# Local attention with a phase mixer on one core: constants in two parts, key reorders on ScalarE, and the order of values, scores and weight transposes

## The chip, the core and the metric

The kernel runs on one core of a Trainium2 chip. The metric is the device time in microseconds of one execution; lower is better. TensorE (PE in the profile) multiplies matrices into PSUM, VectorE (DVE) and ScalarE (ACT) do elementwise work, GpSimd (POOL) issues the loads, SyncE (SP) issues the stores and the transposing DMAs.

## The reference

Four batches, 8 heads, 768 positions, 64 numbers a head. First comes an attention with a local window and eight global positions, then a token and channel mixer on its output.

```python
scores = q @ k.T / sqrt(64)                       # per batch and head
keep   = (col < 8) | ((row - col >= 0) & (row - col < 96))
dist   = where((col < 8) & ~local, 96, |row - col|)
scores = where(keep, scores - slope[head] * dist, -1e9)
x      = softmax(scores) @ v                      # heads side by side: 768 x 512
theta  = x @ w_theta
y      = w_tok_r @ (x * cos(theta)) + w_tok_i @ (x * sin(theta))
u      = x + y
out    = u + relu(u @ w_ch)
```

## The kernel before

Heads are taken in four pairs, and the 768 positions in six tiles of 128. Matmul operands are bf16, sums are float32 in PSUM. There are two large PSUM buffers (`ps_big`, two banks each) and four small ones (`ps_small`), which are handed out in turn.

**Loads.** POOL issues all loads and converts them on the way: q and k of batch 0 by pairs (L72), v of batch 0 in two halves (L78), then `w_theta`, the six blocks of the two token matrices (L158), `w_ch`, then q, k and v of batches 1, 2 and 3. Tile `vn` holds v and, in a 65th column of each head, ones, so that the values' matmul also gives the softmax's sums. `alloc_loads` (L63) writes that column with a DVE memset ahead of the loads.

**Constants.** DVE builds a ramp, the identity `ident`, the distances `dist` with a huge number where the window doesn't reach, zeroes in four score buffers `e_0` to `e_3`, the mask and bias of the global columns (`gmask`, `gbias`), the shift matrices, pi/2, and `zero`, the operand of filler matmuls (`warm`, L174). ACT makes `etab`, the window's factors exp(-slope * dist), one exponential for each of eight heads (L110).

**Attention of a pair.** `prep` (L190) reorders q and k on DVE into `qkn` (two copies, L199), transposes them on PE (L207) and copies the results to `qT` by DVE (L212) and `kT` by ACT (L214). `scores` (L235) works on two tiles at a time (L247), takes the exponential on ACT (L251, L258, L259) and multiplies by `etab` on DVE (L254, L260, L261). `globals_` (L217) does the global columns of all pairs; `vglob` (L266) brings the global rows of v into place, with an ACT copy `vg` (L272). `values` (L275) sums both parts (L292) and divides on DVE (L300, L302) into `x_sb`. `xtrans` (L304) transposes x: on PE with an ACT copy in batch 0 (L312, L313), by a transposing DMA in the others (L306).

**Mixer.** `theta` (L318) multiplies x by `w_theta` (L327), two tiles to a large buffer; ACT takes both sines (L331, L332; cosine is the sine with pi/2 added), DVE multiplies them with x into `zri` (L335). `mix` (L340) runs 12 matmuls for each of six row tiles (L346), and DVE adds x to give u (L351). `utrans` transposes u by DMA (L360), `chan` multiplies by `w_ch` (L371), adds (L374) and stores (L376). The token matrices must stand transposed: `trans_w` (L163) does a row block of both, 12 transposes (L167) and two copies (L168).

**Order.** Batch 0's attention is written out for PE in a fixed order (L424 to L446): preparation of pair p, then scores of pair p-1, each chunk with a filler matmul, globals, the last pair's scores, then values of each pair. Between the values, W blocks 0 to 3 are transposed. After that come theta and mix of batch b, into which `weave` (L406) mixes the attention of batch b+1 by weights; W blocks 4 and 5 are transposed in batch 0's mixing (L463). Outside the fixed stretch a scheduler sets the order on each engine, from its own estimate of times. Each engine works through its queue in that order.

Of the kernel before, what the change touches and what calls it, by code (L numbers as in the profile page):

```python
# [9 lines left out]
FP = mybir.dt.float32  # L10
BF = mybir.dt.bfloat16
# [5 lines left out]
def kernel(  # L17
# [45 lines left out]
    def alloc_loads(b):  # L63
        qk = ld.tile([T, 2, H, NT, D], BF, name="qk")
        vn = ld.tile([T, H, NT, D + 1], BF, name="vn")
        nc.vector.memset(vn[:, :, :, D:D + 1], 1.0)
        loads[b] = (qk, vn)
# [17 lines left out]
    load_v(0, 0, 4)  # L85
    load_v(0, 4, 4)

    ones = const.tile([T, W], FP)
# [14 lines left out]
    far = const.tile([T, W], FP)  # L103
    nc.vector.tensor_scalar(far, dist, 0.0, 1e6, op0=ALU.is_lt, op1=ALU.mult)
    nc.vector.tensor_add(dist, dist, far)
    nc.vector.tensor_scalar(far, dist, float(NL), 1e6, op0=ALU.is_ge, op1=ALU.mult)
    nc.vector.tensor_add(dist, dist, far)
    etab = const.tile([T, H, W], BF)
    for h in range(H):
        nc.scalar.activation(etab[:, h, :], dist, AF.Exp, scale=-slopes[h])  # L110


    NE = 4
    e_bufs = []
    for i_ in range(NE):
        e_t = const.tile([T, 2, NT, 2 * T], BF, name=f"e_{i_}")
        nc.vector.memset(e_t[:, :, :, W:2 * T], 0.0)
        e_bufs.append(e_t)
    e_cnt = [0]

    grel = const.tile([T, T], FP)
    nc.vector.tensor_scalar(grel, ramp[:, 0:T], kmod[:, 0:1], None, op0=ALU.subtract)
    gbias = const.tile([T, 2], FP)
    for hh in range(2):
        for p in range(NP):
            nc.vector.memset(gbias[GS * p:GS * (p + 1), hh:hh + 1], -float(NL) * slopes[2 * p + hh])

    gneg = const.tile([T, 1], FP)  # L130
    nc.vector.tensor_scalar(gneg, grel[:, 0:1], -float(NG), -30000.0, op0=ALU.is_le, op1=ALU.mult)
    nc.vector.tensor_scalar(gbias, gbias, gneg, None, op0=ALU.add)

    gfar = const.tile([T, T], FP)
    nc.vector.tensor_scalar(gfar, grel, float(NL), None, op0=ALU.is_ge)
    gmask = const.tile([T, T], BF)
    nc.vector.scalar_tensor_tensor(gmask, in0=grel, scalar=0.0, in1=gfar, op0=ALU.is_lt, op1=ALU.add)

    shift = const.tile([T, NP, T], BF)
    nc.vector.memset(shift, 0.0)  # L140
    for p in range(NP):
        nc.vector.tensor_copy(out=shift[0:NG, p, GS * p:GS * p + NG], in_=ident[0:NG, 0:NG])

    halfpi = const.tile([T, 1], FP)
    nc.vector.memset(halfpi, HALF_PI)

# [22 lines left out]


    zero = const.tile([T, 512], BF)
    nc.vector.memset(zero, 0.0)  # L172

# [16 lines left out]
    def prep(b, p):  # L190
# [6 lines left out]
        with behind("dve"):  # L197
            for i_ in range(2):
                nc.vector.tensor_copy(out=qkn[:, :, i_].rearrange("p t h d -> p h t d"),  # L199
                                      in_=qk[:, i_, 2 * p:2 * p + 2])  # L200
        qT = att.tile([T, S], BF, name="qT", bufs=6)
# [33 lines left out]
    def scores(b, p, c):  # L235
# [14 lines left out]
        if jt + 2 < NT:  # L250
            nc.scalar.activation(  # L251
                e_t[:, :, jt:jt + 2, 0:W],
                pb[:, :, 0:2 * W].rearrange("p a (j w) -> p a j w", j=2), AF.Exp, scale=scale)
# [194 lines left out]
    for b in range(B):  # L448
# [61 lines left out]
```

The softmax here doesn't subtract the row's maximum and nothing guards it: scores larger than these inputs give would overflow.

## Time and profile before

Three runs gave 200.63, 201.6 and 202.19 us, with a median of 201.6.

| What | Value |
|---|---|
| profiled execution, device time | 201.24 us |
| its span | 199.5 us |
| busy: PE, DVE, ACT, POOL | 173.0, 132.6, 105.0, 27.2 us |
| first scores exponential of batch 0 (L251) | at 14.23 us |
| first sine of batch 0 (`cs`, L331) | at 38.72 us |
| first u of batch 0 to the transposing DMA | at 47.10 us |
| first `chan` matmul (L371) | at 54.46 us |
| first theta matmul of batch 1 (L327) | at 79.99 us |

The page gives busy time by engine, the slices of the span, the DMA queues, the chain of work that ended last, and the costliest groups of instructions. A row of a timeline has the start in us, the length in us, engine, line, operation, what is written from what, the count, and in brackets how long the engine had idled and what ended that. A matmul of 512 columns is shown with 0.38 us but starts every 0.216 us, since matmuls overlap. DMA rows on POOL and SP show the issuing only; the time to landing is told by another view.

### The profile page before, as it was taken

Reading aid. Unit: us, or ns where it says so; the run is one execution under the profiler, and the core shown is the slowest. Engines: PE = TensorE matmul, PEld = TensorE weight load, DVE = VectorE, ACT = ScalarE, POOL = GpSimd, SP = SyncE. Lnnn points to the kernel's source line nnn. Section 1 sums busy time; section 2 is a strip of 40 time slices with the busy share of each in tenths; the row PEclk is TensorE's granted clock in tenths of the full one; section 3 lists DMA queues with packets and bytes.
Section 4 is the critical chain, followed back from the end, with each engine's and each line's share of the span. In section 5 each row is a group of like instructions: output and inputs, shape, how many; then the busy total and the mean of one; then the engine's idle time right before and its main releaser. Section 6 shows DMA issues by size and latency. Waiting matters only on the chain.

```text
span 199.5 us, 3940 instructions
## 1 busy us (share of the span) xinstructions
PE 173.0 (87%) x1610; PEld 87.1 (44%) x1610; DVE 132.6 (66%) x305; ACT 105.0 (53%) x153; POOL 27.2 (14%) x31
## 2 busy tenths in 40 slices
PE   0498789998599899799999999699999997899981
PEld 0154268443353445453345455443444552344430
DVE  7878678177765686996676777677686661753332
ACT  2449956990359553189964431399845312920010
POOL 7991461040110000400000000000000000000000
PEclk9999999999999999999999999999999999999999
DMA  4999999999999999699114437210233845103432
GB/s 66 161 174 168 210 209 206 205 176 166 194 165 188 210 162 183 116 135 138 30 26 118 122 92 108 40 69 37 55 82 100 111 120 123 53 20 100 130 91 105
DMA packets 61345, 24.76 MB, mean 124 GB/s; under 512 B 47504, under 2 KB 58256, under 8 KB 61328
## 3 DMA queue, kind: packets, MB, share of 16 engines
q0 software_dynamic: 35760, 12.85, 66.0%
q1 hardware_dynamic: 25568, 11.67, 26.8%
q8 instruction: 12, 0.20, 0.4%
q14 instruction: 5, 0.04, 0.1%
HBM read 25.69 MB, written 6.29 MB: 160 GB/s over the span
## 4 chain that ended last, share of the span: by engine, by line
PE 61%; DMA 13%; ACT 12%; DVE 9%; issue 3%; ACTq 0%
PE ps L346 27%; DMA uT<-u 11%; PE ps L371 9%; PE pb L327 6%; PE pb L292 6%; PE pb L247 4%; PE ps L207 3%; ACT kT L214 2%; DMA xT<-x_sb 2%; PE ps L177 2%; ACT cs L331 2%; DVE u L351 1%; ACT e_121 L251 1%; PE ps L292 1%; PE ps L167 1%
## 5 line engine op out<-in xcount | busy, mean ns | idle before, releaser
L346 PE MATMUL ps<-zri,w_tokT_151 128*128 128x512 bf16 x144 | 53.9, 380 | 1.2 <-DVE zri L335 1.2
L346 PE MATMUL ps<-zri,w_tokT_152 128*128 128x512 bf16 x144 | 54.0, 379 | 0.1
L374 DVE SCALAR_TENSOR_TENSOR o_sb<-ps,u 128x512 f32<-128x512 f32 x24 | 16.5, 688 | 18.8 <-PE ps L371 18.8
L371 PE MATMUL ps<-w_ch_bf,uT 128*128 128x512 bf16 x96 | 24.7, 379 | 4.1 <-DMA uT<-u 3.3
L327 PE MATMUL pb<-w_theta_bf,xT 128*128 128x512 bf16 x96 | 24.6, 379 | 3.3 <-DMA xT<-x_sb 3.0
L214 ACT COPY kT<-ps 128x768 bf16<-128x768 bf16 x16 | 12.4, 808 | 25.9 <-PE ps L207 25.9
L335 DVE TENSOR_TENSOR zri<-x_sb,cs 128x512 bf16<-128x512 bf16 x48 | 18.2, 421 | 8.8 <-ACT cs L331 7.2
L346 PEld LDWEIGHTS <-w_tokT_151 128*128 128x128 bf16 x144 | 14.0, 97 | 16.9 <-issue 4.4
L351 DVE TENSOR_TENSOR u<-x_sb,ps 128x512 bf16<-128x512 bf16 x24 | 16.4, 684 | 7.0 <-PE ps L346 6.7
L346 PEld LDWEIGHTS <-w_tokT_152 128*128 128x128 bf16 x144 | 14.0, 98 | 12.8 <-issue 2.0
L247 PE MATMUL pb<-qT,kT 64*128 64x224 bf16 x192 | 16.8, 254 | 1.7 <-ACT e_117 L251 0.5
L212 DVE COPY qT<-ps 128x768 bf16<-128x768 bf16 x16 | 14.9, 948 | 2.5 <-PE ps L207 2.5
L177 PE MATMUL ps<-zero 128*128 128x512 bf16 x22 | 8.9, 476 | 8.3 <-DVE zero L172 7.8
L207 PE MATMUL ps<-ident,qkn 128*128 128x128 bf16 x192 | 13.8, 223 | 2.0 <-DVE qkn L199 2.0
L78 POOL DMA_DIRECT2D vn<-in_v_dram x5 | 10.2, 2050 | 35.7 <-DVE rec L300 24.7
L327 PEld LDWEIGHTS <-xT 128*128 128x128 bf16 x96 | 8.8, 98 | 14.1 <-DMA xT<-x_sb 4.1
L207 PEld LDWEIGHTS <-qkn 128*128 128x128 bf16 x192 | 12.1, 100 | 6.4 <-DVE qkn L199 3.8
L371 PEld LDWEIGHTS <-uT 128*128 128x128 bf16 x96 | 8.2, 97 | 14.7 <-DMA uT<-u 6.0
L247 PEld LDWEIGHTS <-kT 64*128 64x128 bf16 x192 | 6.0, 94 | 18.2 <-issue 15.8
L331 ACT ACTIVATE cs<-pb,halfpi 128x1024 bf16<-128x1024 f32 x12 | 13.6, 1131 | 0.5 <-ACT cs L332 0.3
L332 ACT ACTIVATE cs<-pb 128x1024 bf16<-128x1024 f32 x12 | 12.5, 1039 | 0.0
L199 DVE COPY qkn<-qk 128x768 bf16<-128x768 bf16 x32 | 11.5, 411 | 0.8 <-DMA qk<-in_q_dram 0.5
(128 smaller groups left out, 261.8 us busy)
## 6 DMA issues: line engine op xcount, KB each, us to landing
out_dram<-o_sb SPq DMA_DIRECT2D x24, 256.0 KB, 2.2
qk<-in_q_dram POOLq DMA_DIRECT2D x3, 768.0 KB, 17.5
qk<-in_k_dram POOLq DMA_DIRECT2D x3, 768.0 KB, 21.8
vn<-in_v_dram POOLq DMA_DIRECT2D x3, 768.0 KB, 23.3
w_nat<-in_moe_w_tok_r_dram POOLq DMA_DIRECT2D x3, 384.0 KB, 14.7
w_nat<-in_moe_w_tok_i_dram POOLq DMA_DIRECT2D x3, 384.0 KB, 15.9
qk<-in_q_dram POOLq DMA_DIRECT2D x4, 192.0 KB, 5.6
qk<-in_k_dram POOLq DMA_DIRECT2D x4, 192.0 KB, 5.8
```

The lines of the kernel that those rows point to most:

```text
L207: nc.tensor.transpose(ps[:, t_, :], qkn[:, t_, i_].rearrange("p h d -> p (h d)"), ident)
L212: nc.vector.tensor_copy(out=dst, in_=src)
L214: nc.scalar.copy(out=dst, in_=src)
L247: nc.tensor.matmul(pb[:, hh, j * W:j * W + n], lhsT=kT[R, jt * T:(jt + 1) * T], rhs=qT[R, jt * T:jt * T + n], start=True, stop=True)
L292: nc.tensor.matmul(o, lhsT=l_, rhs=r_, start=(i_ == 0), stop=(i_ == len(mms) - 1))
L327: nc.tensor.matmul(pb[:, j, :], lhsT=xT[:, dc, st * T:(st + 1) * T], rhs=w_theta_bf[:, dc, :], start=(dc == 0), stop=(dc == NC - 1))
L331: nc.scalar.activation(cs[:, 0], pb, AF.Sin, bias=halfpi)
L335: nc.vector.tensor_mul(zri[b][:, i_, 2 * c + j_, :].rearrange("p (g d) -> p g d", g=NP), xb[:, :, 2 * c + j_, :], cs[:, i_, j_].rearrange( ...
L346: anchor["pe"] = nc.tensor.matmul(ps, lhsT=w_tokT[wi][:, st, tt * T:(tt + 1) * T], rhs=zri[b][:, wi, st, :], start=(st == 0 and wi == 0), ...
L351: anchor["dve"] = nc.vector.tensor_add(u_sb[b, tt].rearrange("p (g d) -> p g d", g=NP), x_sb[b][:, :, tt, :], ps.rearrange("p (g d) -> p g ...
L371: nc.tensor.matmul(ps_c, lhsT=uT[:, dc, :], rhs=w_ch_bf[:, dc, :], start=(dc == 0), stop=(dc == NC - 1))
L374: nc.vector.scalar_tensor_tensor(o_sb, in0=ps_c, scalar=0.0, in1=u, op0=ALU.max, op1=ALU.add)
```

## The change

Five things differ. The zero operand of the fillers is written first. Constants that are needed late go into a function `constants()`, called after pair 1's preparation; with them goes the memset of batch 0's ones column in `vn`, which so stands after the loads of v in program order. Building `dist` takes three operations in place of five, and `etab` is made by pairs, two exponentials after each preparation. In batch 0 the key's reorder of pairs 0 and 1 is an ACT copy. The last pair's scores are placed between the first values, without fillers. Of the W blocks only block 0 is transposed in the fixed stretch, and at its end; blocks 1 to 5 go into batch 0's mixing, with both copies on DVE. And after the last exponential of each batch's last pair ACT takes the sine of one column into `junk`, so that the table of the sine is loaded there.

```diff
     def alloc_loads(b):
-        nc.vector.memset(vn[:, :, :, D:D + 1], 1.0)
+        if b:
+            nc.vector.memset(vn[:, :, :, D:D + 1], 1.0)
...
     load_v(0, 4, 4)
+    zero = const.tile([T, 512], BF)
+    nc.vector.memset(zero, 0.0)
...
-    nc.vector.tensor_scalar(far, dist, 0.0, 1e6, op0=ALU.is_lt, op1=ALU.mult)
-    nc.vector.tensor_add(dist, dist, far)
-    nc.vector.tensor_scalar(far, dist, float(NL), 1e6, op0=ALU.is_ge, op1=ALU.mult)
-    nc.vector.tensor_add(dist, dist, far)
+    nc.vector.tensor_scalar(far, dist, 0.0, None, op0=ALU.is_lt)
+    nc.vector.scalar_tensor_tensor(far, in0=dist, scalar=float(NL), in1=far, op0=ALU.is_ge, op1=ALU.add)
+    nc.vector.scalar_tensor_tensor(dist, in0=far, scalar=1e6, in1=dist, op0=ALU.mult, op1=ALU.max)
     etab = const.tile([T, H, W], BF)
-    for h in range(H):
-        nc.scalar.activation(etab[:, h, :], dist, AF.Exp, scale=-slopes[h])
+
+    def bias_table(p):
+        for h in (2 * p, 2 * p + 1):
+            nc.scalar.activation(etab[:, h, :], dist, AF.Exp, scale=-slopes[h])
...
+    def constants():
+        for e_t in e_bufs:
+            nc.vector.memset(e_t[:, :, :, W:2 * T], 0.0)
...
+        nc.vector.memset(shift, 0.0)
         for p in range(NP):
+            nc.vector.tensor_copy(out=shift[0:NG, p, GS * p:GS * p + NG], in_=ident[0:NG, 0:NG])
+        nc.vector.memset(loads[0][1][:, :, :, D:D + 1], 1.0)
+        nc.vector.memset(halfpi, HALF_PI)
...
             for i_ in range(2):
-                nc.vector.tensor_copy(out=qkn[:, :, i_].rearrange("p t h d -> p h t d"),
-                                      in_=qk[:, i_, 2 * p:2 * p + 2])
+                (nc.scalar.copy if b == 0 and i_ and p < 2 else nc.vector.tensor_copy)(
+                    out=qkn[:, :, i_].rearrange("p t h d -> p h t d"), in_=qk[:, i_, 2 * p:2 * p + 2])
...
-            nc.scalar.activation(e_t[:, :, jt + 1, 0:T], pb[:, :, W:W + T], AF.Exp, scale=scale)
+            last = nc.scalar.activation(e_t[:, :, jt + 1, 0:T], pb[:, :, W:W + T], AF.Exp, scale=scale).ins
+            if p == NP - 1:
+
+                with tc.issue_after(last):
+                    nc.scalar.activation(junk, halfpi, AF.Sin)
...
         prep(0, 0)
+        bias_table(0)
         warm(2)
         for p in range(1, NP):
             prep(0, p)
+            bias_table(p)
+            if p == 1:
+                constants()
             for c in range(NT // 2):
                 scores(0, p - 1, c)
                 warm(1)
         globals_(0)
         for p in range(NP):
             vglob(0, p)
-        for c in range(NT // 2):
-            scores(0, NP - 1, c)
-            warm(1)
+        scores(0, NP - 1, 0)
         for p in range(NP):
             values(0, p, 0)
             values(0, p, 1)
+            if p < 2:
+                scores(0, NP - 1, p + 1)
             if p:
-                trans_w(p - 1, nc.scalar.copy)
                 xtrans(0, p - 1, nc.scalar.copy)
-        trans_w(3, nc.scalar.copy)
         xtrans(0, NP - 1, nc.scalar.copy)
+        trans_w(0, nc.scalar.copy)
...
-                if b == 0 and g == 1 and tt < 2:
-                    main.append((1536, lambda tt=tt: trans_w(tt + 4)))
+                if b == 0 and g == 1 and tt + 1 < NT:
+                    main.append((1536, lambda tt=tt: trans_w(tt + 1)))
```

More of the change, by code (lines that the diff above doesn't have):

```diff
@@ L108 @@
     etab = const.tile([T, H, W], BF)
-    for h in range(H):
-        nc.scalar.activation(etab[:, h, :], dist, AF.Exp, scale=-slopes[h])
+    def bias_table(p):
+        for h in (2 * p, 2 * p + 1):
+            nc.scalar.activation(etab[:, h, :], dist, AF.Exp, scale=-slopes[h])
     NE = 4
[L114 to L118, printed above, removed]
+    e_bufs = [const.tile([T, 2, NT, 2 * T], BF, name=f"e_{i_}") for i_ in range(NE)]
@@ L119 @@
     e_cnt = [0]
-    grel = const.tile([T, T], FP)
-    nc.vector.tensor_scalar(grel, ramp[:, 0:T], kmod[:, 0:1], None, op0=ALU.subtract)
     gbias = const.tile([T, 2], FP)
-    for hh in range(2):
-        for p in range(NP):
[L128 to L145, printed above, removed]
+    gmask = const.tile([T, T], BF)
@@ new lines @@
+    shift = const.tile([T, NP, T], BF)
+    halfpi = const.tile([T, 1], FP)
+    junk = const.tile([T, 1], FP)
+    def constants():
+        for e_t in e_bufs:
+            nc.vector.memset(e_t[:, :, :, W:2 * T], 0.0)
+        grel = const.tile([T, T], FP, name="grel")
+        nc.vector.tensor_scalar(grel, ramp[:, 0:T], kmod[:, 0:1], None, op0=ALU.subtract)
+        for hh in range(2):
+            for p in range(NP):
+                nc.vector.memset(gbias[GS * p:GS * (p + 1), hh:hh + 1], -float(NL) * slopes[2 * p + hh])
+        gneg = const.tile([T, 1], FP, name="gneg")
+        nc.vector.tensor_scalar(gneg, grel[:, 0:1], -float(NG), -30000.0, op0=ALU.is_le, op1=ALU.mult)
+        nc.vector.tensor_scalar(gbias, gbias, gneg, None, op0=ALU.add)
+        gfar = const.tile([T, T], FP, name="gfar")
+        nc.vector.tensor_scalar(gfar, grel, float(NL), None, op0=ALU.is_ge)
+        nc.vector.scalar_tensor_tensor(gmask, in0=grel, scalar=0.0, in1=gfar, op0=ALU.is_lt, op1=ALU.add)
+        nc.vector.memset(shift, 0.0)
+        for p in range(NP):
+            nc.vector.tensor_copy(out=shift[0:NG, p, GS * p:GS * p + NG], in_=ident[0:NG, 0:NG])
+        nc.vector.memset(loads[0][1][:, :, :, D:D + 1], 1.0)
+        nc.vector.memset(halfpi, HALF_PI)
@@ L168, in trans_w @@
             (copy if wi else nc.vector.tensor_copy)(out=w_tokT[wi][:, :, tt * T:(tt + 1) * T], in_=ps)
-    zero = const.tile([T, 512], BF)
-    nc.vector.memset(zero, 0.0)
     def warm(n):
```

## The prediction

> **What bounds the kernel now.** I read the page's table of slices first: PE is busy in nearly every slice after the tenth, and DMA is full until about 75 us. Then I followed the chain of waits in order of time, and for the stretch that the change touches, from 0 to 80 us, the timelines of ACT, POOL and PE. The chain of waits runs through ACT from 13.5 to 28 us, through PE, DVE and ACT together to 38.7 us, and then mostly through PE, with two long transposing DMAs:
>
> ```profile
> 20.40 0.83 ACT e_119 L251
> ...
> 38.72 1.12 ACT cs L331
> ...
> 47.10 7.31 DMA uT<-u
> 54.46 1.04 PE ps L371 x4
> ```
>
> (Columns: start, length, engine, what.) The ACT timeline of the start-up shows what can be gained there:
>
> ```profile
> 6.33 2.35 ACT L110 ACTIVATE etab<-dist 128x224 bf16<-128x224 f32 x8 [4.31 <-DVE dist L107]
> 12.43 0.80 ACT L214 COPY kT<-ps 128x768 bf16<-128x768 bf16 x1 [3.75 <-PE ps L207]
> ...
> 19.59 0.81 ACT L214 COPY kT<-ps 128x768 bf16<-128x768 bf16 x1
> 20.29 1.74 ACT L251 ACTIVATE e_119<-pb 128x896 bf16<-128x896 f32 x2
> ...
> 24.87 1.78 ACT L251 ACTIVATE e_121<-pb 128x896 bf16<-128x896 f32 x2
> ...
> 37.39 1.28 ACT L331 ACT_TABLE_LOAD   x1
> 38.72 1.11 ACT L331 ACTIVATE cs<-pb,halfpi 128x1024 bf16<-128x1024 f32 x1
> ```
>
> ACT idles twice before its first kT copy (4.31 and 3.75 us, in brackets), then has no idle time until 27.4. The eight etab exponentials lie between the two idle times, so they cost nothing today. The POOL timeline tells when a load has landed, because POOL's own later issues wait for it:
>
> ```profile
> 16.52 0.72 POOL L158 DMA_DIRECT2D w_nat<-in_moe_w_tok_i_dram  x1 [1.61 <-DMA vn<-in_v_dram]
> 20.23 0.76 POOL L161 DMA_DIRECT2D w_ch_bf<-in_moe_w_ch_dram  x1 [3.00 <-DMA vn<-in_v_dram]
> ```
>
> The two loads of batch 0's values are complete at about 16.5 and 20.2 us. Nobody on the path waits for them there today.
>
> **What the Trainium skill says.** "ScalarE: Activation LUTs", What ACT_TABLE_LOAD costs: a switch takes about 1283 ns plus a drain of about 1380 ns. The trace agrees on 1.28 us and shows no drain (load at 37.39, next activation at 38.72), so I use 1.28. "DMA: Bandwidth & Descriptors", Queues, rings and completion order: each DMA engine takes packets from its queues in turn, so that a transpose shares the engines with loads. The trace agrees: uT takes 7.3 to 8.7 us between 47 and 68 us, under the loads, and 2.4 to 3.0 us late in the kernel. "TensorE: Matmul & The Clock Gate", Part 1: the HAM clock gate: TensorE runs at half rate until it has been busy for a window of about 3.4 us, and again after an idle one. The trace agrees on the start: the first eight matmuls at L177 take 3.60 us, 0.45 each, against 0.216 from start to start at L346.
>
> **The change, part by part.**
>
> *Earlier start.* The first key blocks land at 6.7 and 9.1 us (issued at 2.07 and 3.49, landing 4.6 and 5.6 later). ACT copies them; the trace has no such copy from SBUF, so its bounds are DVE's 0.35 (L199) and ACT's 0.80 (L214), and I take 0.80: 9.1 + 0.8 = 9.9. Then kT 0.7, two etab at 2.35/8 = 0.29 each, kT 0.7, two etab: first scores exponential at 12.5, against 14.23 before. Fewer DVE operations for dist and the early zero memset hide beside the wait for the loads. But now two etab stand in each later pair, 0.59 on an ACT that is full: the period of a pair, 3.03 before (14.23, 17.25, 20.29), becomes 3.6. The lead of 1.7 is gone by pair 2.
>
> *The memset of vn.* The ones column of batch 0's vn is now written after the loads, in constants(). In the order of instructions that memset waits for both value loads, and it stands on DVE behind pair 2's qT copy and ahead of pair 3's two qkn copies, the multiplies of pair 1 and pair 3's qT. DVE comes to it at about 18 (pair 0's four multiplies end near 17, qT takes 0.95) and stands until 20.2. Who waits: PE's transposes of pair 3, next on its queue. Memset 0.1, two copies of 0.35 give 21.0; key transposes and semaphore 0.7; kT at 21.75 against 19.59: **+2.2**. One etab before the next exponential, +0.3: e_119's row moves from 20.29 to 22.8. From there to e_121's, globals and vg are unchanged, 4.58: 27.4 against 24.87, **+2.5**.
>
> *Values mixed with scores, three W transposes gone.* Before, e_121 to cs took 38.72 - 24.87 = 13.85. Now: pair 0's values fit behind vg, the second exponential ends at 29.35, the last two at 30.6. The table load and the junk Sin follow (1.28 + 0.2; the Sin of one column has no row, bounds 0.1 to vg's 0.27) and end at 32.1. They are not hidden: xT of pair 0 stands behind them, 32.1 to 32.8, and it holds the one of four small PSUM buffers that pair 3's first values need. Those run 32.9 to 34.0; reciprocals and multiplies 1.17 (27.73 to 28.89 in the trace) give 35.1; six transposes 0.5; xT copy to 36.4; six theta matmuls x 0.216 + 0.25 give cs at 38.0. So 10.6 instead of 13.85, **-3.2**, and cs comes **0.7 earlier**. The removed fillers cost nothing while PE waits for ACT.
>
> *Transposes in mixing.* From cs to the first two u nothing differs but which W block is transposed. So uT goes out 0.7 earlier and, at 7.3, lands at 53.7. What differs is the work queued ahead of the first chan (L371): before 8 mix matmuls and 24 transposes, now 5 and 12. PE therefore stands about 3.5 us instead of 2.07, and that work comes after:
>
> ```profile
> 54.46 1.04 PE L371 MATMUL ps<-w_ch_bf,uT 128*128 128x512 bf16 x4 [2.07 <-DMA uT<-u]
> ```
>
> From this chan to the theta of batch 1 took 79.99 - 54.46 = 25.5. Add 12 transposes for queries and keys x 0.056 = 0.67, three W blocks of 12 x 0.056 = 2.0; take off one mix matmul, 0.2, and the 0.75 wait for uT at 68 us, which no longer comes last; add the vg wait of the next step, 0.8: 28.1. The six copies are on DVE, six x 0.55, covered while PE is ahead. Theta of batch 1: 53.7 + 28.1 = 81.8, **+1.8**.
>
> *Table load drawn forward in batches 1 to 3.* It leaves cs's chain, where it is bare:
>
> ```profile
> 77.69 0.27 ACT L272 CAST vg<-ps 128x130 bf16<-128x130 f32 x1
> ...
> 168.19 1.28 ACT L331 ACT_TABLE_LOAD   x1 [7.85 <-PE pb L327]
> 169.49 1.11 ACT L331 ACTIVATE cs<-pb,halfpi 128x1024 bf16<-128x1024 f32 x1
> ```
>
> But it now stands before pair 3's vg copy, for which PE's values wait: 0.8 in batch 1 (counted above), 0.2 in batches 2 and 3, where three mix matmuls come between. The gain is not 1.28 but PE's idle time behind cs: in batch 1 from 88.05 to 92.38 PE has 3.5 of work, so 0.8; in batch 2 0.5; in batch 3 about 0.7. Net of the vg waits of 2 and 3: **-1.6**.
>
> *Sum:* +1.8 - 1.6 = +0.2. The profiled execution took 201.24 (span 199.5 and 1.74 around it), so 201.4; it lies 0.36 under the median of 201.6, and on that footing the forecast is **201.8 us**.
>
> **The rivals.** *The gate is not repaid* (slower). Step three assumes that taking W's transposes out shortens the stretch by 3.2. If what paces it is the turn of PE, DVE and ACT around the four small buffers, with the table load now in that turn, it shortens by about 1.1, cs comes at 40.1, 1.4 late, and the rest follows: 201.8 + 2.1 = 203.9. It decides from cs later than 39.9. For it: DVE's rows before are nearly full from 27.7 to 35.9. Against it: ACT's two idle times of 0.99 and 0.77 there are waits for W's transposes.
>
> *The W transposes fill waits* (faster). If the chan is not PE's next work, or uT lands sooner because it is issued earlier, the three blocks take the place of the 2.07 and 0.75 waits: 2.6 less, 199.2. For it: PE had 4 us of waits between 47 and 80. Against it: in the new order chan stands earlier, and the blocks come behind it.
>
> *The clock.* A wait of 3.5 us is as long as the window; PE at half rate for one window loses 1.7 to 3.4 us: about 204.3. Against it: after 4.3 us with PE busy 2.38 (from 122.1) L327 ran at full rate.
>
> *The move changes nothing in the start-up*, because loads set it: no, the theta weights and all of q and k land well before they are used.
>
> **How the numbers follow.** Forecast, within 1%: 0.42. Gate not repaid: 0.28; clock: 0.06; with other DVE delays from the six copies, slower by over 1% is 0.36. Filling: 0.22. One per cent is 2.0 us, about what this measurement can tell from no change (three runs spread over 1.6 us). The range takes in filling and gate and part of the clock: 199.0 to 204.8, leaving about one tenth on each side.
>
> **What would show it.** In the new profile: a DVE idle time ended by the landing of vn, near 20 us, with pair 3's kT just after 21.5; cs of batch 0 near 38.0; the first L377 matmul waiting over 3 us for uT; theta of batch 1 near 82; no table load ahead of cs in batches 1 to 3, and vg of pair 3 behind it. The forecast is wrong if the memset does not hold DVE, if cs comes after 39.9 or before 36.5, or if the first chan waits less than 2 us.

## The result and the profile after

Four runs of the changed kernel gave 208.81 to 212.24 us, with a median of 211.31; the kernel before, run beside it, had 201.21. The ratio is 1.0455, with a 95% interval of 1.0349 to 1.0562. The forecast was 201.8, with a range to 204.8. Ratios here leave disturbed executions out, so a ratio can differ a little from the quotient of two medians.

The profiled execution is the slowest of the four: it took 212.24 us (span 210.5), 11.0 us of span more than before, where the ratio makes it 9.2 us. The page's table of slices already shows where. (Each digit is a fortieth of the span, 5.3 us; the clock row is what TensorE was granted, 9 for full.)

```profile
PE   6596998997599999629999999979999997999982
...
PEclk9757559999799999985999999999999999999998
```

Before, the clock row was 9 throughout. (It shows only what the trace has on record: the first eight filler matmuls took 0.43 to 0.45 us each in both kernels, half the full rate, and the row says 9 there.) Now it falls in three places: from 5 to 32 us, near 56 us, and near 95 us. The second and third stand behind a dip in PE's own row. The chain of waits in order of time names those dips (columns as before: start, length, engine, what):

```profile
19.59 0.45 DVE qkn L201
20.08 0.86 PE ps L209 x12
20.96 0.80 ACT kT L216
...
39.07 1.12 ACT cs L337
...
47.47 7.71 DMA uT<-u
55.22 1.64 PE ps L377 x4
56.86 1.28 PE ps L209 x12
...
85.07 0.63 DVE u L357
85.70 0.87 DVE x_sb L308
86.56 0.44 DVE qkn L201
87.01 7.00 DMA xT<-x_sb
94.05 2.31 PE pb L333 x5
```

Four chan matmuls took 1.04 us before and take 1.64 here. The last transposing DMA of batch 1's x takes 7.00 us and ends the chain there; before, the same DMA took 2.8.

The start-up on ACT, which answers to the rows shown of before:

```profile
12.46 1.71 ACT L253 ACTIVATE e_107<-pb 128x896 bf16<-128x896 f32 x2
...
20.96 0.80 ACT L216 COPY kT<-ps 128x768 bf16<-128x768 bf16 x1 [1.53 <-PE ps L209]
...
29.22 0.92 ACT L253 ACTIVATE e_110<-pb 128x896 bf16<-128x896 f32 x1 [1.29 <-PE pb L249]
31.61 0.54 ACT L260 ACTIVATE e_110<-pb 128x448 bf16<-128x448 f32 x1 [1.47 <-PE pb L249]
...
32.45 1.28 ACT L265 ACT_TABLE_LOAD   x1
```

The first exponential is where the prediction put it (12.5). Pair 3's kT is 1.4 us later than before, and ACT then waits for PE twice (1.29 and 1.47), because a pair's 34 value matmuls take 2.03 and 1.98 us in the chain at half clock. The gate behind that late kT is on DVE's timeline:

```profile
19.59 0.43 DVE L201 COPY qkn<-qk 128x768 bf16<-128x768 bf16 x1 [2.87 <-DMA vn<-in_v_dram]
19.74 0.10 DVE L149 MEMSET vn<- 128x48 bf16 x1
```

DVE stood 2.87 us until the values of batch 0 had landed.

To see where the 11.0 us lie, cut the profiled execution at five events. All later kernels are cut the same way (us; "chan" is the first chan matmul of batch 0, "theta 1" and "mix 1" the first theta and mix matmul of batch 1):

| Kernel | to cs | cs to chan | chan to theta 1 | theta 1 to mix 1 | to the end |
|---|---|---|---|---|---|
| before | 38.72 | 15.74 | 25.53 | 12.39 | 107.1 |
| after | 39.07 | 16.15 | 29.59 | 18.86 | 106.8 |
| difference | +0.35 | +0.41 | +4.06 | +6.47 | -0.3 |

So there are two losses, 4.1 us in the stretch that now holds the W transposes and 6.5 around theta of batch 1, and a start-up that in this execution gains nothing. The two losses come back in every run below that keeps what makes them; the start-up's 39.07 does not, as the runs with the memset and the fillers show.

### The profile page after: what moved, and what is told of

Its sections match the earlier page's. It is cut to its first block, busy times and chain, and to the rows that moved or that the text cites. A ratio compares the mean times of both kernels' runs of the same rounds, so it can differ in the third digit from the quotient of the medians.

```text
span 210.5 us, 3934 instructions
## 1 busy us (share of the span) xinstructions
PE 184.0 (87%) x1607; PEld 92.8 (44%) x1607; DVE 132.3 (63%) x305; ACT 105.4 (50%) x156; POOL 26.7 (13%) x31
## 4 chain that ended last, share of the span: by engine, by line
PE 60%; DMA 17%; ACT 10%; DVE 5%; POOL 3%; issue 3%; DVEq 0%; ACTq 0%; POOLq 0%
PE ps L352 24%; PE ps L377 10%; PE pb L333 8%; DMA xT<-x_sb 7%; PE pb L298 5%; DMA vn<-in_v_dram 5%; PE pb L249 5%; DMA uT<-u 5%; PE ps L209 3%; POOL qk L73 3%; PE ps L298 2%; ACT cs L337 2%; PE ps L172 1%; PE pb L227 1%; ACT kT L216 1%
## 5 line engine op out<-in xcount | busy, mean ns | idle before, releaser
L352 PE MATMUL ps<-zri,w_tokT_118 128*128 128x512 bf16 x144 | 55.1, 383 | 0.8 <-DVE zri L341 0.4
L352 PE MATMUL ps<-zri,w_tokT_119 128*128 128x512 bf16 x144 | 54.9, 382 | 0.0
L333 PE MATMUL pb<-w_theta_bf,xT 128*128 128x512 bf16 x96 | 25.2, 393 | 8.2 <-DMA xT<-x_sb 7.2
L377 PE MATMUL ps<-w_ch_bf,uT 128*128 128x512 bf16 x96 | 26.1, 396 | 4.1 <-DMA uT<-u 3.9
L380 DVE SCALAR_TENSOR_TENSOR o_sb<-ps,u 128x512 f32<-128x512 f32 x24 | 16.6, 690 | 20.5 <-PE ps L377 20.4
L209 PE MATMUL ps<-ident,qkn 128*128 128x128 bf16 x192 | 17.0, 248 | 5.4 <-DVE qkn L201 2.3
L209 PEld LDWEIGHTS <-qkn 128*128 128x128 bf16 x192 | 14.4, 112 | 12.2 <-DVE qkn L201 6.7
L352 PEld LDWEIGHTS <-w_tokT_119 128*128 128x128 bf16 x144 | 14.2, 98 | 12.5 <-issue 1.7
L249 PE MATMUL pb<-qT,kT 64*128 64x224 bf16 x192 | 18.9, 279 | 0.8 <-ACT e_109 L253 0.3
L201 DVE COPY qkn<-qk 128x768 bf16<-128x768 bf16 x30 | 10.8, 405 | 6.3 <-DMA qk<-in_q_dram 3.5
L79 POOL DMA_DIRECT2D vn<-in_v_dram x5 | 9.5, 1920 | 33.5 <-DVE rec L306 21.3
L249 PEld LDWEIGHTS <-kT 64*128 64x128 bf16 x192 | 6.5, 97 | 16.2 <-issue 13.7
L308 DVE TENSOR_TENSOR x_sb<-pb,rec 128x768 bf16<-128x768 f32 x12 | 11.5, 954 | 0.2
## 6 DMA issues: line engine op xcount, KB each, us to landing
qk<-in_k_dram POOLq DMA_DIRECT2D x3, 768.0 KB, 20.5
vn<-in_v_dram POOLq DMA_DIRECT2D x3, 768.0 KB, 24.1
```

What stands on the lines that cost most here:

```text
L209: nc.tensor.transpose(ps[:, t_, :], qkn[:, t_, i_].rearrange("p h d -> p (h d)"), ident)
L249: nc.tensor.matmul(pb[:, hh, j * W:j * W + n], lhsT=kT[R, jt * T:(jt + 1) * T], rhs=qT[R, jt * T:jt * T + n], start=True, stop=True)
L333: nc.tensor.matmul(pb[:, j, :], lhsT=xT[:, dc, st * T:(st + 1) * T], rhs=w_theta_bf[:, dc, :], start=(dc == 0), stop=(dc == NC - 1))
L352: anchor["pe"] = nc.tensor.matmul(ps, lhsT=w_tokT[wi][:, st, tt * T:(tt + 1) * T], rhs=zri[b][:, wi, st, :], start=(st == 0 and wi == 0), ...
L377: nc.tensor.matmul(ps_c, lhsT=uT[:, dc, :], rhs=w_ch_bf[:, dc, :], start=(dc == 0), stop=(dc == NC - 1))
L380: nc.vector.scalar_tensor_tensor(o_sb, in0=ps_c, scalar=0.0, in1=u, op0=ALU.max, op1=ALU.add)
```

## The experiments

The main theory at first was that the Sin makes the second loss, the late W blocks the first, and that the start-up loses its gain to the memset and to the clock. Rivals stand in each expectation. One profiled execution of each kernel is read, so a difference in one stretch of a few tenths of a microsecond is not told from chance.

**No Sin.** The changed kernel without the early sine.

```diff
-            if p == NP - 1:
-                with tc.issue_after(last):
-                    nc.scalar.activation(junk, halfpi, AF.Sin)
```

> The changed kernel without the one-column sine after the last exponentials, so the sine table is loaded where it was before. Theory A (order): the early table load is what put the last u of batch 0 ahead of batch 1's last x_sb on DVE, and so the last xT transpose behind uT and under the load of v for batch 3, where it took 7.0 us; without it that xT takes under 4 us, batch 1's first sine comes 4 to 6 us earlier, and the kernel takes 205 to 207 us. Theory B (TensorE's half rate in the start-up makes the loss, and xT's 7 us are covered): 210 or more. Theory C (the sine only exposes its 1.28 us again): 211 to 214.

Measured: 205.64 us, ratio 1.0154 (1.0076 to 1.0233). Theta 1 to mix 1 falls from 18.86 to 11.74, the last xT takes 2.8 us. So in the changed kernel the second loss is gone when the Sin is. The rest to the end grows from 106.8 to 108.8, but TensorE also had half its clock here from 129.7 to 133.1 us, which it had not in the changed kernel. So 2.0 us is the most that the early table load is worth in batches 2 and 3; the kernel before with and without the Sin, below, differs there by 0.8.

**Memset first.** The ones column of `vn` written ahead of the loads again.

```diff
-        if b:
-            nc.vector.memset(vn[:, :, :, D:D + 1], 1.0)
+        nc.vector.memset(vn[:, :, :, D:D + 1], 1.0)
...
-        nc.vector.memset(loads[0][1][:, :, :, D:D + 1], 1.0)
```

> The changed kernel with batch 0's ones column written ahead of the loads, as before. Theory A (the wait of DVE for the value loads costs the start-up its gain): kT of pair 3 comes at 19 to 20 us, cs of batch 0 1 to 2 us earlier than 39.07, total 1 to 2 us less than the changed kernel. Theory B (half rate of TensorE sets the start-up anyway): kT of pair 3 moves, cs moves by less than 0.5 us, and so does the total.

Measured: 210.81 us, ratio 1.0357 (1.0235 to 1.0479). Pair 3's kT comes at 19.27 instead of 20.96. The memset is shown to be the gate. cs comes at 36.21, 2.9 us earlier than in the changed kernel's profile, but the gate is not all of that. Three kernels below keep the memset and the start-up as they are: the one with the third buffer for the values, the one with the wait for uT filled, and the one with u behind x_sb. ACT's instructions up to cs are the same and in the same order. In them cs comes at 37.72, 36.94 and 37.61, although pair 3's kT is no earlier (21.84, 20.95 and 21.74). This is ACT in the last of the three:

```profile
21.74 0.80 ACT L216 COPY kT<-ps 128x768 bf16<-128x768 bf16 x1 [2.21 <-PE ps L209]
...
30.74 1.28 ACT L265 ACT_TABLE_LOAD   x1
...
32.14 1.48 ACT L319 COPY xT<-ps 128x768 bf16<-128x768 bf16 x2
...
37.61 1.11 ACT L337 ACTIVATE cs<-pb,halfpi 128x1024 bf16<-128x1024 f32 x1 [0.65 <-PE pb L333]
```

So the gate costs 1.7 to 2.6 us at kT and 0.7 to 1.5 at cs. The other 1.3 to 2.1 us belong to the changed kernel's own profiled execution: TensorE had half its clock there from 21.4 to 31.6 us, and only for 3.4 us, from about 20.5 to 23.9, in those three.

The ratio falls by 0.01, about 2 us, with intervals that overlap. cs to chan grows from 16.15 to 17.00 (uT now takes 8.57 us), chan to theta 1 to 30.39, and the last xT still takes 6.9. What is won ahead of cs is mostly spent on the way to theta 1.

**Clock held.** More fillers in the start-up.

```diff
-        warm(8)
+        warm(19)
         prep(0, 0)
         bias_table(0)
-        warm(2)
+        warm(8)
```

> The changed kernel with 19 filler matmuls ahead of pair 0 in place of 8, and 8 behind it in place of 2, so that TensorE stays busy until the first scores. Theory A (half rate costs): granted clock full from 10 to 30 us, where it was 0.57 to 0.60, cs of batch 0 1 to 2.5 us earlier, total 1 to 3 us less. Theory B (the value loads' wait sets the start-up): the clock is full, cs moves by less than 0.7 us.

Measured: 209.43 us, ratio 1.037 (1.031 to 1.0431). TensorE has its full clock from 6.0 to 23.1 us, then half of it to 29.9, behind the gate that is still there (0.66 on the mean from 20 to 30). With eight fillers it had half of it from 7.7 to 18.0 us in the changed kernel, and the three kernels named above are as slow there: the twelve transposes of pair 2 near 14 us take 1.49 to 1.59 us in all four, and 0.83 here. So the fillers do hold the clock. But they push the first exponential from 12.46 to 13.89, and cs comes at 38.60. That is only 0.5 earlier than in the changed kernel, as theory B had it, and 0.9 to 1.7 later than in those three. With half the clock until 17 us cs can still come at 36.9 to 37.7; 10 us of half rate behind 21 us go with a cs that is 1.3 to 2.1 us later.

**W early.** The changed kernel with the W blocks transposed between the values of batch 0, as before.

```diff
             if p:
+                trans_w(p - 1, nc.scalar.copy)
                 xtrans(0, p - 1, nc.scalar.copy)
+        trans_w(3, nc.scalar.copy)
         xtrans(0, NP - 1, nc.scalar.copy)
-        trans_w(0, nc.scalar.copy)
...
-                if b == 0 and g == 1 and tt + 1 < NT:
-                    main.append((1536, lambda tt=tt: trans_w(tt + 1)))
+                if b == 0 and g == 1 and tt < 2:
+                    main.append((1536, lambda tt=tt: trans_w(tt + 4)))
```

> The changed kernel with the W blocks transposed where they were before: 0 to 3 between the values, 4 and 5 in mixing. Theory A (moving them cost more in mixing than it gave in the start-up): cs of batch 0 2 to 3 us later than 39.07, but theta of batch 1 starts 1 to 2 us earlier than 84.8; total 1 to 2 us less than the changed kernel. Theory B (their move pays): total 1 to 3 us more.

Measured: 203.87 us over 20 runs (200.68 to 207.96; the profiled execution is the fastest), ratio 1.0034 (0.9999 to 1.007). cs is later, 40.62, but chan to theta 1 is 23.56, and although the Sin is in, the last xT takes 2.8 us. By the ratio that saves about 8.5 us, where theory A had 1 to 2. So with W early the Sin does no harm: the second loss needs both edits.

**Each of the two alone, in the kernel before.** First the W blocks late and nothing else; then the Sin and nothing else. Their diffs are those of the change.

> The kernel before with one part of the change alone: the W_tok blocks 1 to 5 are transposed one by one among the mixing units of batch 0, block 0 at the end of the start-up. Theory A (the late blocks cost by themselves: 36 transposes more between cs and the theta of batch 1, the first chan queued earlier, so a longer wait for uT and TensorE at half rate behind it): cs of batch 0 1 to 2 us earlier than 38.72, the first L371 waits over 3 us for uT, the stretch from cs to the first theta of batch 1 grows from 41.3 to 44 or more, and the time is 203.5 to 206. Theory B (they only cost together with the rest of the change, where the delayed first keys and the Sin have already used up the slack): within 1% of the kernel before, 200 to 203.5, the earlier cs pays for the transposes.

Measured: 203.91 us, ratio 1.0163 (1.0095 to 1.023). Theory A, except that cs, at 37.85, is 0.9 us earlier and not 1 to 2: cs to theta 1 takes 45.3, chan to theta 1 29.18, and on PE's timeline

```profile
54.01 1.89 PE L371 MATMUL ps<-w_ch_bf,uT 128*128 128x512 bf16 x4 [3.69 <-DMA uT<-u]
...
58.73 0.94 PE L167 MATMUL ps<-ident,w_nat 128*128 128x128 bf16 x12
```

PE stands 3.69 us for uT, then does chan at half rate, and a W block comes only after that.

> The kernel before with the Sin of one column behind the last exponentials of every batch, and nothing else of the change. Theory A (the Sin alone makes the loss near 85 us: the multiply that makes u is then placed ahead of the last x_sb on DVE, so the last xT of batch 1 is issued behind the load of batch 3's values and takes about 7 us): the last xT takes 6.5 to 7.5 us instead of 2.8, PE waits 3 to 4 us for it and runs at half rate after that, and the time is 204.5 to 207. Theory B (the Sin hurts only because the late W blocks had moved u and the value load near to each other; the drawn-forward table load is otherwise a small gain as the prediction had it): 199.5 to 202, xT 3 us or less.

Measured: 200.52 us over 20 runs, ratio 0.9936 (0.991 to 0.9962). Here theory A fell. Alone, the Sin is a gain of 1.3 us, and the last xT takes 3.0. The two parts by themselves cost 3.3 and gain 1.3; together with the rest they cost 9.2 by the ratio.

**What collides.** In the changed kernel POOL issues the load of batch 3's values at 85.48, and that last xT goes out at 87.01, 1.53 us behind. With the values in three buffers that load is issued at 50.51.

```diff
-        vn = ld.tile([T, H, NT, D + 1], BF, name="vn")
+        vn = ld.tile([T, H, NT, D + 1], BF, name="vn", bufs=3)
...
-        o_sb = moe.tile([T, DM], FP, name="o_sb", bufs=4)
+        o_sb = moe.tile([T, DM], FP, name="o_sb", bufs=3)
```

> The changed kernel with three buffers for the values in place of two (and three for the output tile in place of four, for space), so that batch 3's values are loaded near 45 us and not near 85. Order of DVE and SP is as in the changed kernel. Theory A (xT's 7.0 us come from sharing the DMA engines with that load): the last xT of batch 1 takes 2.4 to 3.2 us, PE's wait ahead of its theta falls from 4.1 us to under 1, no half rate behind it, and the time is 204.5 to 207.5. Theory B (the transpose is slow for another reason, such as the uT issued just before it on the same queue, or u ahead of x_sb costs by the order itself): xT keeps 6 us or more, or the wait keeps 3 us, and the time stays at 209 to 211.5.

Measured: 207.26 us, ratio 1.0215 (1.0156 to 1.0274). The last xT takes 2.6 us, and theta 1 to mix 1 falls from 18.86 to 14.67. But a wait of 2.36 us and a stretch at half clock remain. They belong to the xT before it, issued at 81.34, which took 6.2 us: the load of batch 3's k, issued at 62.50, landed only 21.0 us later, at 83.5. So the load of the values is what slowed the last transpose, as theory A had it; PE's wait is above its range. That the load of k slowed the transpose before it fits these times, but no run tests it.

**Does the start-up gain by itself?** Memset first, W early, no Sin, clock held: what stays is the split of the constants, the key copies on ACT, and the values mixed with the last scores.

> The changed kernel with four things changed back or mended: the ones column of vn is written ahead of the loads, the W blocks are transposed in the start-up as before, the Sin is left out, and more filler matmuls keep TensorE busy from 5 to 20 us (as in the run with the clock held). What stays is the split of the constants, the key copies on ACT and the values mixed with the last scores. Theory A (the start-up itself gains once nothing downstream eats it): kT of pair 3 near 18 to 19.5, cs of batch 0 at 37 to 38.5, theta of batch 1 at 77.5 to 79.5, and the time 198 to 200.5. Theory B (what is gained ahead of cs is lost again in the wait for uT, which ends when the loads let it): theta of batch 1 at 79.5 to 81.5 and the time 200.5 to 203.

Measured: 201.45 us over 12 runs, ratio 1.0004 (0.9968 to 1.004). cs comes at 37.91, but cs to theta 1 takes 42.5 against 41.3 before. Theory B held: the 0.8 us won ahead of cs are gone by theta 1.

**What the wait for uT costs.** In the changed kernel, 14 matmuls with zeros open the sum of the first chan, so that PE has work while it waits.

```diff
+        fill = 14 if (b, tt) == (0, 0) else 0
+        for i_ in range(fill):
+            nc.tensor.matmul(ps_c, lhsT=zero[:, 0:T], rhs=zero, start=(i_ == 0), stop=False)
         for dc in range(NC):
...
-                             start=(dc == 0), stop=(dc == NC - 1))
+                             start=(dc == 0 and not fill), stop=(dc == NC - 1))
```

> The changed kernel with 14 matmuls with zeros (3.0 us at full rate) as the first part of the first chan's sum in batch 0, where PE stands 3.68 us for uT. They add zero. Theory A (the stand costs more than itself: TensorE runs at half rate for about 3.4 us after it, worth 1.5 to 2): granted clock 1.00 from 54 to 60, the stretch from chan to the theta of batch 1 falls from 29.6 to 27.5 to 28.2, and the time is 207.5 to 210.5 (less, if the transposes near 85 us fall differently). Theory B (the half rate there is hidden behind DVE's copies of the W blocks): that stretch stays at 29 or more, and the time within 1% of the changed kernel.

Measured: 207.81 us, ratio 1.0272 (1.0197 to 1.0347). PE's timeline in this run:

```profile
49.24 3.19 PE L378 MATMUL ps<-zero 128*128 128x512 bf16 x13
53.50 1.04 PE L380 MATMUL ps<-w_ch_bf,uT 128*128 128x512 bf16 x4 [1.07 <-DMA uT<-u]
54.37 0.83 PE L209 MATMUL ps<-ident,qkn 128*128 128x128 bf16 x12
```

Chan is back at 1.04 us, the clock is full from 54 to 60, and chan to theta 1 falls from 29.59 to 27.64. Work that adds nothing saved 1.95 us there; the six other runs with W late and an empty wait have 29.2 to 30.4 in this stretch. (The ratio falls by more, 3.7 us. Part of that may be the start-up, which the filling doesn't touch: cs came at 36.94 here.) The other stretch, theta 1 to mix 1, is unchanged at 18.55, as is its xT (7.2 us).

**W blocks in the wait.** The kernel before, W late, but blocks 2 to 5 ahead of the first chan; then the same with the Sin.

```diff
-                if b == 0 and g == 1 and tt < 2:
-                    main.append((1536, lambda tt=tt: trans_w(tt + 4)))
+                if b == 0 and (tt, g) in ((0, 1), (1, 0), (1, 1), (1, 2), (2, 0)):
+                    blk = {(0, 1): 1, (1, 0): 2, (1, 1): 3, (1, 2): 4, (2, 0): 5}[tt, g]
+                    main.append((1536, lambda blk=blk: trans_w(blk)))
```

> The kernel before with the W blocks late, as in the run that made this change alone, but blocks 2 to 5 drawn forward so that all their transposes stand ahead of the first chan, in the time in which PE waits for uT. Theory A (late blocks cost because three of them come behind that wait): PE's wait falls from 3.69 us to under 2.5, no half rate behind it, chan to theta of batch 1 falls from 29.2 to 25 to 27, and the time is 199.5 to 201.8, which is the filling that the prediction had as a rival. Theory B (they cost through DVE, which copies them and then is late with u and the query and key copies): the first u comes later, chan starts at 55 or later, and the time stays at 202.5 to 205.

Measured: 202.38 us over 12 runs, ratio 0.9971 (0.9936 to 1.0005), against 1.0163 with W behind chan. The wait ahead of the first chan is gone and the clock is full there. By the ratios, the place behind the wait is all that late W blocks cost. The trace does not show that saving: the profiled execution, 203.75, is one of the slower ones, its span of 202.0 is that of W behind chan (201.8), the wait comes back at 78 us as 2.98 us for a later uT, and chan to theta 1 is 28.48, where theory A had 25 to 27. In that execution the waiting is moved, not removed, and the time of the twelve lies above theory A's range.

> The run with the W blocks ahead of the first chan, and the Sin behind the last exponentials as well. Theory A (with the attention of batch 1 back in its old place, the Sin is the small gain that it is in the kernel before): 198 to 200.5, the last xT of batch 1 lands in 3 us. Theory B (the late blocks keep u near to the last values of batch 1, so that the xT falls behind the value load): xT 6 us or more, PE waits over 3 us near 90, and the time is 203 or more.

Measured: 209.04 us, ratio 1.0316 (1.0234 to 1.0398), xT 7.05 us, PE waits 4.13. Theory B: with W late, in both places that were tried, the Sin brings the collision back.

> The changed kernel with the ones column written ahead of the loads, the W blocks transposed in the start-up as before, and the clock held by more fillers; the Sin stays. Theory A (the parts add up when W is early: the start-up 0, the Sin -1.3): 199 to 201, the last xT in 3 us, cs near 38. Theory B (the earlier start brings the last xT behind the value load again): 203 or more, xT 6 us or more.

Here W is early, the memset first and the clock held. Measured: 200.57 us, ratio 0.989 (0.9817 to 0.9964), xT 2.7 us. Theory A: with W early the parts add up. This kernel, the one before with the Sin alone, and the last one below are the fastest of all; their intervals overlap.

**One instruction on DVE.** What differs near 85 us between kernels with and without the collision is the order of a multiply, which makes x_sb, and an add, which makes u. This run is the changed kernel, whole, with the last u of batch 0 put behind the last x_sb of batch 1.

```diff
-        if g == NT // 2 - 1:
+        if g == NT // 2 - 1 and (b, tt) == (0, NT - 1):
+            pss["u"] = ps
+        elif g == NT // 2 - 1:
...
         weave(main, pre + side, 0.3 if b == 0 else 0.0)
+        if b == 0:
+            u_sb[0, NT - 1] = moe.tile([T, DM], BF, name="u", bufs=4)
+            with tc.issue_after(anchor["x"]):
+                anchor["dve"] = nc.vector.tensor_add(
```

(`anchor["x"]` is the latest multiply that makes x_sb.)

> The changed kernel whole, the Sin included, with one DVE instruction in another place: the add that makes the last u of batch 0 stands behind the multiply that makes the last x_sb of batch 1, and no longer ahead of it. Theory A (the Sin hurts through this order alone): the last xT is issued 0.6 to 0.7 us behind the load of batch 3's values instead of 1.53, and lands in 2.6 to 3 us; the stretch from the theta of batch 1 to its first mix falls from 18.9 to 12 to 13.5, and the time is 203.5 to 206. Theory B (the table load ahead of vg, and all that it delays, hurts by itself near 85 us): the stretch stays at 15 or more and the time is over 207.

Measured: 206.1 us, ratio 1.019 (1.0094 to 1.0287), 0.1 above theory A's range, and without a difference from the run without the Sin that the intervals would show. DVE's timeline in this run:

```profile
83.98 0.26 DVE L306 RECIPROCAL rec<-pb 128x12 f32<-128x12 f32 x1 [1.71 <-PE pb L298]
84.13 0.10 DVE L67 MEMSET vn<- 128x48 bf16 x1
84.28 0.96 DVE L308 TENSOR_TENSOR x_sb<-pb,rec 128x768 bf16<-128x768 f32 x1
85.16 0.68 DVE L485 TENSOR_TENSOR u<-x_sb,ps 128x512 bf16<-128x512 bf16 x1
```

And in the changed kernel:

```profile
84.82 0.26 DVE L306 RECIPROCAL rec<-pb 128x12 f32<-128x12 f32 x1 [1.71 <-PE pb L298]
84.97 0.10 DVE L67 MEMSET vn<- 128x48 bf16 x1
85.01 0.69 DVE L357 TENSOR_TENSOR u<-x_sb,ps 128x512 bf16<-128x512 bf16 x1
85.61 0.95 DVE L308 TENSOR_TENSOR x_sb<-pb,rec 128x768 bf16<-128x768 f32 x1
```

The value load of batch 3 is issued about half a microsecond after that memset in both, and the two transposes go out in the order of u and x_sb. First this run, then the changed kernel:

```profile
84.64 2.22 POOL L79 DMA_DIRECT2D vn<-in_v_dram  x1 [21.30 <-DVE rec L306]
85.27 1.21 SPq L312 DMA_TRANSPOSE xT<-x_sb  x1
86.57 1.23 SPq L368 DMA_TRANSPOSE uT<-u  x1
...
85.48 2.22 POOL L79 DMA_DIRECT2D vn<-in_v_dram  x1 [21.29 <-DVE rec L306]
85.72 1.19 SPq L366 DMA_TRANSPOSE uT<-u  x1
87.01 1.26 SPq L312 DMA_TRANSPOSE xT<-x_sb  x1
```

With u in between, xT is issued 1.53 us behind the load, without it 0.63, and the transpose takes 7.0 or 2.8 us. The load still slows one of the two: now it is uT, which is issued 1.94 us behind the load and takes 7.55 us where it took 2.43. But for that one PE stands only 0.69 us, at 94.17, and for xT it stood 4.08:

```profile
94.05 2.31 PE L333 MATMUL pb<-w_theta_bf,xT 128*128 128x512 bf16 x5 [4.08 <-DMA xT<-x_sb]
```

One swap of 0.69 us takes theta 1 to mix 1 from 18.86 to 12.59.

**All mended.** Every part of the change, with the memset first, the clock held, the W blocks ahead of the first chan, and the last u behind x_sb.

> The changed kernel with every part of the change kept and each mended: ones column ahead of the loads, more fillers from 5 to 20 us, the late W blocks 2 to 5 ahead of the first chan, and the last u of batch 0 behind the last x_sb of batch 1. Theory A (the three costs are all there is): cs at 35.5 to 37.5, theta of batch 1 at 80 to 82.5, last xT in 3 us, and the time is 198 to 201. Theory B (what is won ahead of chan is lost in a later wait for uT, near 78 us, as in the run with W ahead of chan): a wait of 2 us or more there, theta of batch 1 at 82.5 or later, and 201 to 204.

Measured: 201.14 us over 20 runs, ratio 0.9941 (0.9908 to 0.9973), cs at 35.86, theta 1 at 81.06, xT 2.8 us. Both theories are partly right. The three costs are gone and the kernel beats the one before, by 0.6%, but of the 2.9 us won ahead of cs none reaches theta 1 (79.99 before), and the wait of 3.34 us for a later uT is there as theory B said:

```profile
77.37 1.04 PE L377 MATMUL ps<-w_ch_bf,uT 128*128 128x512 bf16 x4 [3.34 <-DMA uT<-u]
```

The cuts of these runs, in us, for the stretches that the text reads:

| Kernel | to cs | cs to chan | chan to theta 1 | theta 1 to mix 1 | to the end |
|---|---|---|---|---|---|
| no Sin | 37.79 | 16.40 | 29.41 | 11.74 | 108.8 |
| W early | 40.62 | 16.64 | 23.56 | 12.57 | 105.5 |
| before, W late | 37.85 | 16.16 | 29.18 | 11.66 | 107.0 |
| before, Sin | 39.81 | 15.91 | 24.28 | 12.77 | 106.3 |
| third buffer | 37.72 | 16.79 | 29.59 | 14.67 | 108.3 |
| wait for uT filled | 36.94 | 16.56 | 27.64 | 18.55 | 106.3 |
| W ahead of chan | 36.82 | 18.06 | 28.48 | 11.29 | 107.3 |
| u behind x_sb | 37.61 | 16.76 | 29.60 | 12.59 | 107.2 |
| all mended | 35.86 | 18.06 | 27.14 | 12.46 | 105.9 |

## Why the prediction was wrong

*Earlier start: right.* First exponential at 12.46 (12.5 predicted); ACT's copies from SBUF took 0.83 (0.80 taken).

*The memset of vn: right in kind and in size.* DVE was free at 19.59, not 20.2, so kT came at 20.96 rather than 21.75 and pair 2's first exponentials at 21.95 rather than 22.8. In the runs with the third buffer and with u behind x_sb kT came at 21.84 and 21.74.

*Values mixed with scores: right, though not in the changed kernel's own profile.* The run with u behind x_sb, the same ahead of cs, follows the forecast nearly term by term: kT of pair 3 at 21.74 (21.75 predicted), the xT copies behind the junk Sin at 32.14 (32.1), cs at 37.61 (38.0). In part that is luck, for the step took the matmuls at full rate, and TensorE had half its clock there until 17 us and from 20.7 to 24.1. In the profiled changed kernel cs came at 39.07: the half rate went from 21.4 to 31.6 us, and pairs' values took 2.0 us each in the chain. The clock rival looked for that behind one wait at 54 us and priced one window; neither it nor the step asked what the earlier start does to the clock. The eight fillers now run from 1.2 to 4.6 us, PE is busy for only 2.67 of the 5 us from 5 to 10, and from 10 to 15 it is granted 0.50; before, they ran from 7.75 and led straight into the work. Why the half rate behind 21 us lasts 10.2 us in one execution and 3.4 in others of the same start-up is open.

*Transposes in mixing: right in kind, too small.* Two terms were mis-sized. The first is ahead of chan: the step let uT go out 0.7 us earlier and take 7.3, so that it lands at 53.7. In the three kernels of the same start-up uT did go out 1.0 to 1.8 us earlier than before, but took 8.1 to 8.4 us, and the first chan came at 53.50 to 54.51, against 54.46 before. In the profiled changed kernel uT went out 0.37 later, took 7.71, and chan came at 55.22. The second is behind it. Predicted from chan to theta 1: 28.1 against 25.5, so +2.6; measured 29.59, +4.1. The predicted wait was 3.5, the measured 3.68. What was left out is that PE runs at half rate after this wait; filling it gave 1.95 us back, and 29.59 less 1.95 is 27.64, within half a microsecond of the 28.1. As the clock rival had it, such a wait can cost a window as well. The argument against that rival was a wait of 4.3 us with PE busy for 2.38 of it, after which L327 ran at full rate. That compared a wait which was half filled with one that was empty.

*Table load drawn forward: the step that failed.* The prediction had -1.6 for it. In the kernel before, where only this is added, the step nearly holds: it had 1.6 less the 0.8 for vg, the gain is 1.3, and the rest to the end, with batches 2 and 3, is 0.8 shorter (0.8 predicted there). The vg of pair 3 waits as it said. With the order mended, chan to mix 1 is 1.0 longer with the Sin than without it; the step had 0.8, all of it ahead of theta 1, where 0.2 was found. What the step did not look at is the order on DVE and SP near 85 us, which the scheduler draws from its estimates and which the compiled program shows. With W late, the last u of batch 0 and the last x_sb of batch 1 are neighbours on DVE; with the Sin the values wait, and u goes first. That puts xT 1.53 us behind a load. The transpose takes 4.2 us more and PE stands 4.08 us. Then it has half its clock to 99.9 us (0.51 from 94 to 100). Of the 6.3 us by which the swap shortens theta 1 to mix 1, 4.6 are PE's waits (1.00 and 4.08 us against 0.52); by estimate the other 1.7 are mostly the half rate. The prediction moved a table load past vg and counted vg; it did not count the DMAs that wait on the values behind it.

*The rivals.* In the changed kernel's profile the gate was not repaid by cs, by 0.35 us; in the three kernels of the same start-up it was, by 1.0 to 1.8 us. So that rival's price of 2.1 is not what was seen. The filling of waits is real, but only where W is put ahead of chan (1.0163 to 0.9971), as the argument against it said. The clock was the rival that happened, in three places instead of one.

*What the sum became.* Predicted +0.2; measured +11.0 of span: +0.8 to chan where -0.8 was expected, +4.1 to theta 1, +6.5 to mix 1, -0.3 after.

What stays open: why what is won ahead of cs does not reach theta 1 even where all is mended. The runs show only where it is spent: the first uT takes longer when it goes out earlier (8.54 us from 44.25 in the kernel with all mended, 7.31 from 47.10 before), and PE waits for uT ahead of 54 or 78 us.

## What to carry to other kernels

Before a small reordering is priced by engine time, print the order of the instructions and DMAs it leads to, and ask of each DMA on the path which load is issued ahead of it. An empty wait of TensorE can cost twice: price it as the wait plus a stretch of half rate behind it, and look for work that can stand in it. The parts of a change need not add up. Here W late costs 3.3 us alone and the Sin -1.3; the start-up as it stands costs about 2.0, an estimate from W early against the Sin alone (1.0034 and 0.9936). That makes 4.0, and together they cost 9.2. So test parts in pairs, not only one by one. And before a stretch of one profile is explained, look at the same stretch in another execution: cs at 39.07 was not what this start-up usually does here.

## What the runs showed of the hardware

A transposing DMA from SBUF to SBUF that was issued 0.16 to 0.64 us after the software-issued load of batch 3's values (768 KB) took 2.7 to 3.0 us in ten kernels; issued 1.53 us after it, 6.9 to 7.2 us in five. Those were xT. The uT beside it follow the same line: 2.4 to 2.7 us when issued 0.24 us behind the load, in the same five, and 7.3 to 7.8 us when issued 1.94 us behind it, in seven of the ten. Nothing between 0.64 and 1.53 us was measured. "DMA: Bandwidth & Descriptors", Queues, rings and completion order, in the Trainium skill says that an engine takes packets from its queues in turn, which agrees with the slow case; that going out within about half a microsecond of the load escapes it is only this case's measurement. POOL's issue of that load lasts 2.22 us, so in both cases the transpose is issued while the load is still being handed over.

TensorE lost half its clock behind an empty wait of 3.68 us. "TensorE: Matmul & The Clock Gate", HAM oscillation — how this bites in real kernels, in the Trainium skill describes this for waits on DMA, and names idle gaps of over about 3.4 us. The runs here are not so simple: half rate also followed waits of 2.22 and 2.57 us (start-up mended with the Sin, and four parts undone), and none followed 3.34 and 2.98 us (all mended, and W early). What the sixteen traces show is a grid. Within a trace the recorded clock changes only on steps of 3.41 us, and the grid lies differently from trace to trace. Of the full-rate steps ahead of 190 us in which PE was busy less than 0.41 of the time, all 24 were followed by half rate; from 0.41 to 0.53, 6 of 17; above that, 6 of 739, all near 20 to 26 us. So where a wait falls on the grid matters: the 3.34 us straddle two steps that are 0.61 and 0.41 busy, and the 2.22 us lie in one that is 0.34 busy. Half rate then lasted one step (55.5 to 58.9 us in the changed kernel) or more (93.1 to 99.9, two).
